# Gated attention and dropless experts on one core: two loads divided into column pieces

## The chip, the core and the metric

The kernel runs on one core of a Trainium2 chip. The core has a matrix engine, TensorE (PE), with a queue for weight loads (PEld); VectorE (DVE), ScalarE (ACT) and GpSimd (POOL); and SyncE (SP), which here does nothing but issue transfers. The engines run separate instruction queues in order and wait for each other through semaphores. The metric is the time of one execution on the device, in microseconds (us), and lower is better.

## What is computed

First a gated linear attention over a complex state, then a routed expert layer, top 1 of 8, all in float32:

```python
mag = np.sqrt(a_re * a_re + a_im * a_im)
scale = np.minimum(mag, 0.999) / (mag + 1e-06)
for t in range(S):                     # S = 768, B = 4, H = 8, D = 48
    new_re = ar * S_re - ai * S_im     # ar, ai: the scaled gates at t
    new_im = ar * S_im + ai * S_re
    S_re, S_im = new_re + k_t v_t^T, new_im
    y[:, :, t] = q_t S_re
x = y as (3072 tokens, 384)
logits = x @ w_gate                    # 8 experts
e = argmax(logits); g = softmax(logits)[e]
out = g * (relu(x @ w1[e]) @ w2[e])    # w1: 384 x 1024, w2: 1024 x 384
```

## The kernel before, in words

**Attention.** Time is cut into six stretches of 128 steps. Within a stretch the gates become cumulative decays and angles, and the recurrence becomes matrix products. Its stages are placed by hand-set priorities (the table WHEN), and a scheduler orders each engine's instructions from them. The fast path uses an approximation of the gates that holds only in a range: a_re above 0.61 and above |a_im|. So all gates are read a second time and tested.

**The range check** is `in_range(j)`, j = 0 to 5. A piece j is a tile of 128 rows by RW = 1536 columns of a_re and one of a_im (tile name `rc`; 768 KB each, 6 KB per row). Two reductions on DVE (line 926, output `junk`) read both tiles. The pool `rp` has two buffers of each tile, so piece j + 2 can be loaded only when both reductions of piece j are done. The results are used once, in `verdict()`, before the last expert. Piece j is called behind expert place j + 1 in the text, but the scheduler is free to put their transfers and reductions where it sees room. In the built program the first five rc transfers stand ahead of expert place 1's weights on SP's queue.

**Experts.** The eight experts are sorted by their number of tokens into "places" 0 to 7, with room for 448, 416, 416, 408, 400, 384, 376 and 360 tokens (CAPS). For each place:

- `load_w(i)` (lines 588 to 602) reads the expert's number and issues its weights on SP: `wa`, the first weights, 128 x 3 x 1024 elements, 1536 KB, and `wb`, the second, 1536 KB. For place 0 wa is one transfer over 128 rows. For places 1 to 7 it is four transfers of 32 rows each (384 KB, runs of 4 KB); the rows are permuted to suit a transpose of 32 x 32 blocks on DVE. wb has runs of 1.5 KB. There are two sets of buffers, even and odd places: wa of place i + 2 can go out when the first layer of place i is done, wb when its second layer is done. Place 1's weights wait until place 0's tokens have been turned ("rows first").
- `gather(i)` (line 616) collects the tokens' rows by indirect transfers that GpSimd issues (tile `xg`); `turn(i)` transposes them (on PE for place 0, line 646, on DVE for the others, line 636).
- `expert(i)` runs the first layer (matmuls into `hps`, eight h tiles of 128 columns of w1, 3 steps each, two matmul records per step), empties each PSUM tile with a ReLU, even h tiles on DVE (line 691), odd ones on ACT (line 689), in four PSUM buffers; then the second layer (matmuls into `yps`), the scaling by the gate on DVE (line 711), and `scatter`, an indirect write to the output by GpSimd (line 658).

Place 0 is in two parts: its first two token tiles run while attention ends; the rest, its tail of 192 columns, runs at about 298 us. Every transfer that SP issues carries one of eight semaphores in turn, and it is held until the transfer that used the same semaphore before it has landed. So at most eight are under way. If the range check fails or an expert has more tokens than its place holds, a general path runs; with these inputs it does not.

Of the kernel before, what the change touches and what calls it, by code (L numbers as in the profile page):

```python
# [17 lines left out]
SYNC = mybir.DependencyInfo(mybir.DependencyClass.Sync, mybir.DependencyReason.DATA)  # L18
# [6 lines left out]
T_MAX = 1.5  # L25
SQ = 1
Q4 = 32
CAPS = (448, 416, 416, 408, 400, 384, 376, 360)


# [8 lines left out]
def kernel(  # L39
# [12 lines left out]
    nc = tc.nc  # L52
# [4 lines left out]
    E, _, F = w1.shape  # L57
# [22 lines left out]
    def const(shape, name, dt=FP):  # L80
        return cp.tile(shape, dt, name=name)

    def iota(pattern, name, base=0, cm=0):
# [16 lines left out]
        out=last, in_=ones, pattern=[[0, P]], base=-(P - 1), channel_multiplier=1, compare_op=OP.is_ge, fill=0.0  # L100
# [26 lines left out]
    for a in range(4):  # L127
        nc.gpsimd.memset(quarter[a * Q4 : (a + 1) * Q4], float(a))

# [340 lines left out]
    caps = const([P, E], "caps")  # L470
    for i, c in enumerate(CAPS):
        nc.gpsimd.memset(caps[:, i : i + 1], float(c))
# [112 lines left out]
    def tiles(i):  # L585
        return -(-CAPS[i] // P)

    def load_w(i, after=None):
        o = own0 if i == 0 else owner[:, i : i + 1]
        ev = nc.sync.value_load(o[0:1, 0:1], min_val=0, max_val=E - 1)  # L590
        wa = EP[i % 2].tile([P, KD, F], FP, tag="wa", name="wa")
        parts = [(slice(0, P), w1[ds(ev, 1)].rearrange("o (k p) f -> p (o k) f", p=P))]
        if i >= SQ:
            w = w1[ds(ev, 1)].rearrange("o (a k j) f -> a j (o k) f", a=4, k=KD)
            parts = [(slice(a * Q4, (a + 1) * Q4), w[a]) for a in range(4)]
        for p, w in parts:
            ins = nc.sync.dma_start(out=wa[p], in_=w)
            if after is not None:
                tc.add_manual_dep(ins.ins, after.ins.name, SYNC, reason="rows first")
        wb = EP[i % 2].tile([P, KF, DM], FP, tag="wb", name="wb")  # L600
        nc.sync.dma_start(out=wb, in_=w2[ds(ev, 1)].rearrange("o (i p) d -> p (o i) d", p=P))
        T["w", i] = wa, wb

    def gather(i, t0, t1, rows=N):

        if t0 == 0:
            T["xg", i] = EP[i % 2].tile([P, CT * DM], FP, tag="xg", name="xg")
        c1 = min(CAPS[i], t1 * P)
        if i < SQ:
            view, w = xd[0:rows, :], DM  # L610
            parts = [(min(P, c1 - t * P), t, tok[:, i, t : t + 1]) for t in range(t0, t1)]
        else:
            view, w = xd.rearrange("n (a c) -> (n a) c", a=4), DM // 4
            parts = [(P, j, tok4[:, i, j // 4, j % 4 : j % 4 + 1]) for j in range(4 * t0, -(-c1 // Q4))]
        for m, (n, j, ap) in enumerate(parts):
# [12 lines left out]
    def turn(i, t0, t1, ps, end=None):  # L628

        xg = T["xg", i]  # L630
        if t0 == 0:
            T["xt", i] = EP[i % 2].tile([P, KD, CAPS[0]], FP, tag="xt", name="xt")
        c0, c1 = t0 * P, min(CAPS[i], t1 * P)
        if i >= SQ:
            j1 = -(-c1 // Q4)
            T["turned"] = nc.vector.transpose(
                out=T["xt", i][:, :, c0 : j1 * Q4].rearrange("p k (j s) -> p j k s", s=Q4),
                in_=xg[:, c0 // Q4 * (DM // 4) : j1 * (DM // 4)].rearrange("p (j k x) -> p j k x", x=Q4, k=KD),
            )
            behind(T["turned"], [T["held"]])  # L640
            return
        for d in range(KD):
            tp = ps.tile([P, 512], FP, tag="tp", name="tp")
            for t in range(t0, t1):
                n = min(P, CAPS[i] - t * P)
                ins = nc.tensor.transpose(
# [130 lines left out]
    for hp in range(HP):  # L777
        for i in range(2):
            nc.sync.dma_start(
                out=back[i * 64 : i * 64 + D, hp, DD:], in_=w_gate[hp * DD + i * D : hp * DD + (i + 1) * D, :]  # L780
# [84 lines left out]
    for g in range(NT):  # L865
        u, b = divmod(g, B)
        if b % HB == 0 and u + 1 < NU:
            put(g, load_qkv, u + 1, b // HB)
        if b in (1, 2) and u + 3 < NU:
            put(g, load_gates, u + 3, *HS[b - 1])  # L870
        if b == 0 and u in GROUPS:
            tc.cur_priority = 4000 + int((g + 1) * 200)
            T["second"] = route(*GROUPS[u])
        if u == NU - 1 and b == 0:
            gates_only.close()
            tc.cur_priority = 4000 + int((g + 1) * 200)
            T["second"] = route(NU - 2, NU - 1)
            put(g + 1, table, "natural_log_exp_and_others")
            put(g + 1, T["second"])
            put(g + 1, first_place)  # L880
            EP[0] = pool2("e0", 1, side="right", reuse_waits="tile")
            EP["y"] = pool2("y0", 2, side="right", reuse_waits="tile")
            put(g + 1, load_w, 0)
            put(g + 1, gather, 0, 0, EARLY, (NU - 1) * B * P)
        ahead(g)
        at(when("products"), products, g + 1) if g else None
        at(when("results0"), results, g, 0)
        at(when("results1"), results, g, 1)
        at(when("state"), state, g)
        at(when("evict"), evict, g)  # L890
        at(when("scores0"), scores, g + 1, 0)
        at(when("scores1"), scores, g + 1, 1)
        at(when("outer"), outer, g + 1)
        at(when("finish"), finish, g)
# [21 lines left out]
    RW = N * DM // P // NR_  # L916
    inr = const([P, 2 * NR_], "inr")

    def in_range(j):
        a = [rp.tile([P, RW], FP, tag=f"rc{i}", name=f"rc{i}") for i in range(2)]  # L920
        for t, src in zip(a, (a_re, a_im)):
            s = src.rearrange("b h t d -> (b h t d)").rearrange("(p f) -> p f", p=P)
            nc.sync.dma_start(out=t, in_=s[:, j * RW : (j + 1) * RW])
        junk = rp.tile([P, RW], FP, tag="junk", name="junk", bufs=1)
        for i, (op, sc) in enumerate(((OP.max, A_MIN), (OP.mult, -1.0))):
            stt(
                out=junk, in0=a[1], scalar=sc, in1=a[0], op0=op, op1=OP.is_lt,
                accum_out=inr[:, 2 * j + i : 2 * j + i + 1],
            )
# [19 lines left out]
    DRAINS = (3, 6)  # L949
    turn(0, EARLY, tiles(0), psG)  # L950
    load_w(1, T["turned"])
    for i in range(E):
        t0 = EARLY if i == 0 else 0
        if i == E - 1:
            verdict()
        if i + 1 < E:
            gather(i + 1, 0, tiles(i + 1))
        expert(i, t0, tiles(i), psH, psO, yp, (lambda: turn(i + 1, 0, tiles(i + 1), psG)) if i + 1 < E else None)
        if i in DRAINS:
            drain()  # L960
        if i + 2 < E:
            load_w(i + 2)
        if 1 <= i <= NR_:
            in_range(i - 1)
# [4 lines left out]
    with tc.If(nc.values_load(flag[0:1, 1:2], min_val=0, max_val=P * (NC + 1)) > 0):  # L969
# [16 lines left out]
        with tc.If(bad_gates > 0):  # L986
            with tc.tile_pool(name="fb", bufs=1) as fb:
# [8 lines left out]
                w = [fb.tile([P, TS, DG], FP, name=f"w{i}") for i in range(3)]  # L996
                yt = fb.tile([P, TS, D], FP, name="yt")
                yo = fb.tile([B * H, TS, D], FP, name="yo")
                with tc.For_i(0, S // TS, 1) as iv:
                    for i in range(4):  # L1000
                        sl = slice(i * B * H, (i + 1) * B * H)
                        for t, a in zip(src, (q, k, a_re, a_im)):
                            nc.sync.dma_start(
                                out=t[sl],
                                in_=a[:, :, ds(iv * TS, TS), i * DG : (i + 1) * DG].rearrange("b h t d -> (b h) t d"),
# [34 lines left out]
                    for b in range(B):  # L1040
                        nc.sync.dma_start(
                            out=xf[ds(iv * TS + b * S, TS), :].rearrange("t (h e) -> h t e", h=H),
                            in_=yo[b * H : (b + 1) * H],
# [134 lines left out]
        with tc.For_i(0, cnti, 1) as iv:  # L1178
            ev = nc.sync.value_load(gown[0:1, ds(iv, 1)], min_val=0, max_val=E - 1)
            wa = ro.tile([P, KD, F], FP, tag="wa", name="wa")  # L1180
# [8 lines left out]
                out=xg, out_offset=None, in_=xf[:, :], in_offset=bass.IndirectOffsetOnAxis(ap=ti, axis=0)  # L1189
# [13 lines left out]
            for f in range(KF):  # L1203
# [4 lines left out]
                out=out,  # L1208
                out_offset=bass.IndirectOffsetOnAxis(ap=ri, axis=0),
                in_=y,  # L1210
# [40 lines left out]
```

## Time and profile before

| | |
|---|---|
| runs | 563.99 us median of 3 (560.99 to 564.17) |
| the profiled execution | 561.03 us; its span 559.3 us |
| mean granted clock of TensorE | 0.991 |
| DMA, whole span | 73.49 MB in 167,735 packets, 131 GB/s |
| SP's queue of transfers | 162,792 packets, 63.12 MB, 52.4% of 16 engines' span |
| GpSimd's queue | 4,896 packets, 9.77 MB, 5.9% |
| wa: transfers | 28 of 384 KB and 1 of 1536 KB |
| rc: transfers | 12 of 768 KB |
| rc reductions on DVE | 12, median 1748 ns, from 292.3 to 443.2 us |

The span in forty slices of 14 us each; a digit is the busy share in tenths:

```profile
DVE  5378687788789888785565221251442412212210
ACT  6877988876588874553200010111101102000000
POOL 3000000000000000001058555707347064370101
PEclk9989989999999999999999999999999899999999
DMA  9977691938655826503468966753865444650001
```

Up to about 270 us it is attention, with all engines at work; then come the experts, where DVE and ACT are mostly idle and GpSimd gathers and scatters. The chain of work that ended last says the same by line: "PE yps L69 16.4%; PE hps L69 13.7%; issue 3.5%", of the part of it that can be followed back.

How to read it: an engine's busy share is an average over stages. PE's matmul ends are modelled, and a few records of evictions or matmuls may be missing. "remote" or "issue" as the releaser of a wait means that the profile shows nothing for it.

### The profile page before, as it was taken

Reading aid. Unit: us, or ns where it says so; the run is one execution under the profiler, and the core shown is the slowest. Engines: PE = TensorE matmul, PEld = TensorE weight load, DVE = VectorE, ACT = ScalarE, POOL = GpSimd, SP = SyncE. Lnnn points to the kernel's source line nnn. Section 1 sums busy time; section 2 is a strip of 40 time slices with the busy share of each in tenths; the row PEclk is TensorE's granted clock in tenths of the full one; section 3 lists DMA queues with packets and bytes.
Section 4 is the critical chain, followed back from the end, with each engine's and each line's share of the span. In section 5 each row is a group of like instructions: output and inputs, shape, how many; then the busy total and the mean of one; then the engine's idle time right before and its main releaser. Section 6 shows DMA issues by size and latency. Waiting matters only on the chain. (4 is left out here: it accounts for less than half of the span.)

```text
span 559.3 us, 8295 instructions
## 1 busy us (share of the span) xinstructions
PE 523.6 (94%) x3154; PEld 370.8 (66%) x3154; DVE 289.6 (52%) x585; ACT 214.3 (38%) x323; POOL 132.7 (24%) x161
## 2 busy tenths in 40 slices
PE   3889979999999999999998999899899899999996
PEld 3666858878888898888766555455454455555663
DVE  5378687788789888785565221251442412212210
ACT  6877988876588874553200010111101102000000
POOL 3000000000000000001058555707347064370101
PEclk9989989999999999999999999999999899999999
DMA  9977691938655826503468966753865444650001
GB/s 164 187 102 103 112 142 22 180 60 168 116 86 115 150 55 140 74 30 139 174 222 222 265 196 137 252 133 73 307 142 189 144 112 148 135 171 18 26 2 41
DMA packets 167735, 73.49 MB, mean 131 GB/s; under 512 B 149053, under 2 KB 160343, under 8 KB 167688
## 3 DMA queue, kind: packets, MB, share of 16 engines
q1 hardware_dynamic: 162792, 63.12, 52.4%
q0 software_dynamic: 4896, 9.77, 5.9%
q8 instruction: 27, 0.44, 0.3%
q14 instruction: 20, 0.16, 0.1%
HBM read 63.34 MB, written 9.73 MB: 131 GB/s over the span
## 5 line engine op out<-in xcount | busy, mean ns | idle before, releaser
L69 PE MATMUL hps<-xt,wa 128*128 128x416 f32 (+7 forms) x432 | 136.8, 472 | 8.8 <-issue 4.2
L69 PE MATMUL yps<-wb,ht 128*128 128x384 f32 (+6 forms) x464 | 134.1, 487 | 0.0
L69 PEld LDWEIGHTS hps<-xt,wa 128*128 128x128 f32 x432 | 79.9, 192 | 62.7 <-issue 32.0
L616 POOL DMA_INDIRECT xg<-xd,tok x92 | 94.8, 1030 | 88.5 <-PE tp L332 40.6
L69 PEld LDWEIGHTS yps<-wb,ht 128*128 128x128 f32 (+6 forms) x464 | 75.1, 175 | 55.8 <-issue 8.6
L689 ACT ACTIVATE ht<-hps 128x416 f32<-128x416 f32 (+7 forms) x36 | 16.7, 467 | 151.7 <-PE hps L69 103.9
L711 DVE TENSOR_SCALAR y<-yps,gate 128x384 f32<-128x384 f32 (+1 forms) x23 | 14.2, 618 | 93.2 <-PE yps L69 76.5
L658 POOL DMA_INDIRECT out_dram<-y,row x28 | 29.2, 1044 | 118.6 <-DVE y L711 100.9
L69 PE MATMUL at<-qt,kt 96*128 96x128 f32 x384 | 53.9, 280 | 0.7 <-DVE am L340 0.7
L691 DVE TENSOR_SCALAR ht<-hps 128x416 f32<-128x416 f32 (+7 forms) x36 | 18.8, 527 | 68.6 <-PE hps L69 41.8
L261 POOL DMA_DIRECT2D ai<-cd x4 | 3.4, 839 | 211.0 <-ACT R L175 100.6
L69 PEld LDWEIGHTS at<-qt,kt 96*128 96x128 f32 x384 | 47.7, 192 | 4.5 <-issue 1.1
L69 PE MATMUL yt<-am,v 128*48 128x128 f32 x384 | 42.7, 281 | 0.6 <-DVE am L340 0.6
L340 DVE TENSOR_TENSOR am<-at,tri 128x512 f32<-128x512 f32 x48 | 33.0, 688 | 18.6 <-PE at L69 18.5
L721 ACT COPY z<-yps 32x384 f32<-32x384 f32 (+3 forms) x13 | 6.1, 470 | 84.2 <-PE hps L69 58.0
L69 PE MATMUL yt<-qt,G 96*48 96x128 f32 x320 | 35.7, 274 | 0.0
L332 PE MATMUL tp<-ident,K 128*96 128x128 f32 x192 | 33.5, 284 | 1.3 <-DVE K L323 1.1
L69 PEld LDWEIGHTS dk<-v,K 128*96 128x96 f32 x320 | 32.9, 168 | 2.1 <-issue 1.0
L69 PE MATMUL dk<-v,K 128*96 128x48 f32 x320 | 33.5, 244 | 0.2 <-DVE G L371 0.2
L332 PE MATMUL tp<-ident,Q 128*96 128x128 f32 x192 | 33.4, 277 | 0.0
L334 ACT COPY kt<-tp 96x512 f32<-96x512 f32 x48 | 27.9, 581 | 11.0 <-PE tp L332 10.8
L334 ACT COPY qt<-tp 96x512 f32<-96x512 f32 x48 | 28.2, 587 | 4.2 <-PE tp L332 4.2
(170 smaller groups left out, 667.2 us busy)
## 6 DMA issues: line engine op xcount, KB each, us to landing
wb<-in_moe_w_dram SPq DMA_DIRECT2D x8, 1536.0 KB
wa<-in_moe_w_dram SPq DMA_DIRECT2D x28, 384.0 KB
q<-in_q_dram SPq DMA_DIRECT2D x12, 384.0 KB
k<-in_k_dram SPq DMA_DIRECT2D x12, 384.0 KB
v<-in_v_dram SPq DMA_DIRECT2D x12, 384.0 KB
xd<-x SPq DMA_DIRECT2D x24, 192.0 KB
rc<-in_a_re_dram SPq DMA_DIRECT2D x6, 768.0 KB
rc<-in_a_im_dram SPq DMA_DIRECT2D x6, 768.0 KB
```

The lines of the kernel that those rows point to most:

```text
L69: T["mm"] = nc.tensor.matmul(o, lhsT=lhsT, rhs=rhs, start=start, stop=stop, skip_group_check=True)
L261: nc.gpsimd.dma_start(out=T["ai", u][0:1, b0:b1].rearrange("p b h d -> p (b h d)"), in_=cd[1, u - 1 : u, b0 * DM : b1 * DM], accum_op=OP.add,)
L332: nc.tensor.transpose(out=tp[0:DD, j], in_=X[:, hg * 4 + j], identity=ident)
L334: nc.scalar.copy(out=t[0:DD], in_=tp[0:DD])
L340: tt(out=am, in0=at, in1=bc(tri, 1, 4), op=OP.mult)
L616: ins = nc.gpsimd.indirect_dma_start(out=T["xg", i][0:n, j * w : (j + 1) * w], out_offset=None, in_=view, in_offset=bass.IndirectOffsetOnA ...
L658: ins = nc.gpsimd.indirect_dma_start(out=out, out_offset=bass.IndirectOffsetOnAxis(ap=row[0:n, i, t : t + 1] if to is None else to[0:n], a ...
L689: nc.scalar.activation(out=ht[:, f, c0:c1], in_=ps, func=AF.Relu)
L691: T["held"] = ts(out=ht[:, f, c0:c1], in0=ps, scalar1=0.0, scalar2=None, op0=OP.max)
L711: ts(out=y[0:n], in0=ps[0:n], scalar1=g, scalar2=None, op0=OP.mult)
L721: nc.scalar.copy(out=z[j * w : j * w + n], in_=ps[j * w : j * w + n])
```

## The change

A constant CUT = 256 columns, 1 KB of float32, is introduced. Each wa transfer becomes four, one for each 256 of its 1024 columns; for places 1 to 7 the loop over column pieces is outside, the one over the four row groups inside, so all rows of the first 256 columns go before the next 256. Each rc transfer of 1536 columns becomes six. Every new wa transfer carries the same dependence on the turned rows, where there was one. The loads of wb, the buffers and all compute instructions are unchanged.

```diff
+CUT = 256
...
     def load_w(i, after=None):
...
-        for p, w in parts:
-            ins = nc.sync.dma_start(out=wa[p], in_=w)
-            if after is not None:
-                tc.add_manual_dep(ins.ins, after.ins.name, SYNC, reason="rows first")
+        for c in range(0, F, CUT):
+            for p, w in parts:
+                ins = nc.sync.dma_start(out=wa[p, :, c : c + CUT], in_=w[:, :, c : c + CUT])
+                if after is not None:
+                    tc.add_manual_dep(ins.ins, after.ins.name, SYNC, reason="rows first")
...
     def in_range(j):
...
-            nc.sync.dma_start(out=t, in_=s[:, j * RW : (j + 1) * RW])
+            for c in range(0, RW, CUT):
+                nc.sync.dma_start(out=t[:, c : c + CUT], in_=s[:, j * RW + c : j * RW + c + CUT])
```

The transfers per execution are then 116 for wa (98,304 bytes each for places 1 to 7, 384 KB for place 0) and 72 for rc (128 KB each).

## The prediction

> **What bounds the kernel now.** I read the busy shares first, then TensorE's (PE's) timeline from the first expert on, then SP's, because the edit lies in two loads that SP issues, and last the engines that empty PSUM. The page's first line names the bottleneck:
>
> ```profile
> PE 523.6 (94%) x3154; PEld 370.8 (66%) x3154; DVE 289.6 (52%) x585; ACT 214.3 (38%) x323; POOL 132.7 (24%) x161
> ```
>
> PE is busy 523.6 of 559.3 us, so a transfer counts only where PE waits for it, directly or through another engine. PE's timeline (start us, length us, engine, line, operation, tiles, shape, count; idle before it and what ended that):
>
> ```profile
> 290.66 0.27 PE L646 MATMUL tp<-ident,xg 128*128 128x128 f32 x1
> 291.72 0.74 PE L646 MATMUL tp<-ident,xg 64*128 64x64 f32 x3 [0.79 <-DMA xg<-xd,tok]
> 292.87 0.33 PE L646 MATMUL tp<-ident,xg 128*128 128x128 f32 x1 [0.41 <-issue]
> ...
> 316.81 17.03 PE L69 MATMUL hps<-xt,wa 128*128 128x416 f32 x48
> ```
> ```profile
> 422.70 10.34 PE L69 MATMUL hps<-xt,wa 128*128 128x400 f32 x30
> 435.35 8.01 PE L69 MATMUL hps<-xt,wa 128*128 128x400 f32 x18 [2.31 <-ACT ht L689]
> ...
> 460.18 9.95 PE L69 MATMUL hps<-xt,wa 128*128 128x384 f32 x30
> 471.48 6.07 PE L69 MATMUL hps<-xt,wa 128*128 128x384 f32 x18 [1.35 <-ACT ht L689]
> ...
> 492.87 15.32 PE L69 MATMUL hps<-xt,wa 128*128 128x376 f32 x48
> ```
>
> Place 1 (416 columns) runs its 48 first-layer matmuls without a gap in 17.03 us, place 6 (376) in 15.32. Place 4 (400) takes 20.65 us, 422.70 to 443.35 where the chain of waits starts its second layer; in proportion to place 1 it would be 16.4. So measured place 2 (350.68 to 369.91) loses 2.2 us, place 3 (386.75 to 405.87) 2.4, place 4 4.3, place 5 (460.18 to 477.55) 1.6: 10.5 us, the largest idle pool of the expert stages. None of it waits for weights. PSUM is emptied late:
>
> ```profile
> 434.79 0.90 ACT L689 ACTIVATE ht<-hps 128x400 f32<-128x400 f32 x2 [7.11 <-issue]
> ```
> ```profile
> 430.00:431.00 1.00, 1.00 (x5) 0.56 (x4) 0.93 (x3) 0.00 (x0) 0.69 (x2) 1.00 1.02 381
> ...
> 434.00:435.00 1.00, 0.00 (x0) 0.00 (x0) 0.18 (x1) 0.21 (x1) 0.00 (x0) 1.00 0.99 393
> ...
> 437.00:438.00 1.00, 1.00 (x2) 0.37 (x2) 0.19 (x1) 0.00 (x0) 0.00 (x0) 0.50 0.02 6
> ```
>
> ACT takes h tile 1 at 434.79, although six matmuls at 0.34 us each put its end near 426.8. In these rows (window; length; busy PE, weight load, DVE, ACT, POOL; granted clock; DMA share; GB/s) the DMA engines are full at 381 to 393 GB/s, PE stands still in 434 to 435, and afterwards its granted clock is 0.50. What is in flight is on SP's timeline:
>
> ```profile
> 283.89 0.45 SPq L923 DMA_DIRECT2D rc<-in_a_re_dram  x1
> 284.36 0.34 SPq L923 DMA_DIRECT2D rc<-in_a_im_dram  x1
> 284.76 0.42 SPq L923 DMA_DIRECT2D rc<-in_a_re_dram  x1
> ...
> 299.86 3.33 SPq L597 DMA_DIRECT2D wa<-in_moe_w_dram  x4
> ...
> 426.20 0.40 SPq L601 DMA_DIRECT2D wb<-in_moe_w_dram  x1
> 426.69 0.64 SPq L923 DMA_DIRECT2D rc<-in_a_re_dram  x1
> 427.38 0.43 SPq L923 DMA_DIRECT2D rc<-in_a_im_dram  x1
> 443.38 1.90 SPq L597 DMA_DIRECT2D wa<-in_moe_w_dram  x4
> ```
>
> Behind place 4's evictions lie wb (1536 KB) and a pair of gate pieces (768 KB each); behind place 5's only a wb. The evictions are late in both, longer where the gate pieces are.
>
> **The change part by part.** Bytes, buffers and arithmetic stay. *SP's instructions.* wa becomes 4 instead of 1 for place 0, and 16 instead of 4 for places 1 to 7: 87 more. The gate pieces become 72 instead of 12: 60 more. At 0.47 us apiece (1.90 / 4; the gate rows start 0.47 and 0.40 apart) that is 69 us more of SP, in an engine that mostly waits.
>
> *wa of places 1 to 7.* 16 x 0.47 = 7.5 us per load instead of 1.9. Here a rule speaks against the change. The row: four parts of 384 KB leave SP in 1.90 us, so several are under way at once. The Trainium skill, page "DMA: Bandwidth & Descriptors", section "Rules for kernel authors", says to use 1 MiB or more per DMA and that small ones pay mostly overhead; its fit in "Anatomy of one DMA" (taken on GpSimd's path) is 2.0 us plus bytes / 436e3. For a part of 98,304 bytes I estimate 2.23 us from it, 36 us for 16 in a row, the whole of a place (386.75 to 422.70): wa and wb would not fit, and the kernel would be slower by tens of us. But the program gives SP's transfers eight semaphores in turn and holds a transfer only until the eighth before it has landed: eight at a time make 36 / 8 = 4.5 us, below the 7.5 us of issue. I take the row. Slack covers 7.5 us everywhere: wa of place 3 starts at 333.87 and is needed at 386.75. The tightest is place 1: 299.86 + 7.5 + 2 = 309.4 against 316.81, and at the slow pace of its four parts (3.33 / 4 = 0.83) it ends at 315.2. wb of place 1 then leaves at 307.4 to 313.2 instead of 303.24; it is needed at 333.68. Cost 0.
>
> *Place 0.* Three more transfers put wb 1.2 us later, at 261.2; the x write behind it starts at 262.34 and the first use of wb is at 278.54. Cost 0.
>
> *Order.* In the built program the queues of PE, ACT and POOL keep their order. On SP the gate parts slide behind later loads: all but the first part of piece 2 still go behind place 3's load; piece 4's first buffer is free only when piece 2's reductions are done, and DVE now runs those behind place 3's transposition (near 409 instead of 369.75). SP stands there with wa of place 5 queued behind: 409.3 + 7 x 0.47 + 7.5 = 420, in place of 407.8; needed at 460.18, and wb of place 5 goes at 426.20 as before. Likewise wa of place 6 waits behind piece 5 for piece 3's reductions (near 446.8): 446.8 + 12 x 0.47 + 7.5 = 460, needed at 492.87, wb due at 462.33. Cost 0. On DVE the twelve reductions (1.75 us each) only change places; the pair between two evictions of place 5 is 3.5 us beside four PSUM buffers, so I cost it at 0; uncovered, 1 us.
>
> *PE's waits.* Each first layer now waits for its weights at four h tiles instead of one, on up to four or five semaphores. Nearest row: place 6 starts with a wait on four, and its 15.32 us against 17.03 x 376 / 416 = 15.4 show nothing. Value 0; upper bound, if each of some 24 new waits cost 0.1 us, 2.4.
>
> *The gather at 291.72.* The gate pieces 0 and 1 leave SP within 2 us (from 283.89) and fill the DMA engines while GpSimd's gather for place 0 is on its way; PE waits 0.79 us for it, and 0.41 behind it. In parts, SP releases 128 KB per 0.45 us, 291 GB/s, against the 381 to 393 that fill the engines, so the gather finds gaps. Between 0 and -1.2 us; I take -0.8. The part after: DVE's first reduction at 292.31 needs 12 parts: 283.89 + 12 x 0.45 + 2 = 291.3. Just in time.
>
> *Late evictions.* Gate parts beside place 4 shrink from two pieces to five parts (640 of 1536 KB; the rest waits for a buffer), beside place 3 from three pieces to two. Place 4 loses 2.7 us more than place 5, which has only wb: that is the most the gate pieces can be worth there. But wb, unchanged, is late-making alone. Bounds -4 and, if more transfers make it worse, +1.5; I take -1.0, nearer to place 5.
>
> Sum: -0.8 - 1.0 = -1.8 us. The profiled execution took 561.03 us (span 559.3), so it becomes 559.2. The median of the runs, 563.99, lies 2.96 above that execution; carried over, 562.2.
>
> **The rivals.** *Slower: SP's throttle starves the gate reduction.* The eight-in-flight rule bites if parts take more than about 0.6 us each. At the 0.83 seen for wa of place 1, the 24 parts from 283.89 end at 303.8 and land near 305.8. DVE's third reduction stands between the first two evictions of place 0's tail and would hold the queue from about 300 to 307.6; PE, with four PSUM buffers, stops near 305, and the fourth reduction (1.75 us) follows before the next eviction. Price 3 to 7 us, at 6 with the gather's gain lost: 570 in terms of the median. For it: the 3.33 us. Against it: 0.47 in every other row. It decides from 0.6 us per part.
>
> *Faster: the long runs are what makes PSUM late.* If 1 KB runs let GpSimd's gathers and the evictions through, places 2 to 4 fall to place 5's loss: 2.2 + 2.4 + 4.3 - 3 x 1.6 = 4.1, with 1.2 from the gather and 2.4 from place 0's tail, 298.49 to 308.83 (48 matmuls of 192 columns in 10.3 us, 7.9 in proportion to place 1): -7.7, 556.3. For it: place 4 against place 5. Against it: wb's rows of 1.5 KB are left as they are, and place 5 suffers without any changed transfer.
>
> *Nothing.* The edit is off PE's path altogether, and the losses are tied to what stays: 564.
>
> **How the numbers follow.** This kernel's runs spread from 560.99 to 564.17, so about 1% is what can be told from no change: below 558.4 faster, above 569.6 slower. The forecast and *nothing* together 0.55; the faster rival 0.20; slower 0.25, the throttle and unknown costs of 147 more transfers (PE's waits at their bound included). The range leaves out the tail of the faster rival beyond 555 and of the slower beyond 572; the likeliest case alone is 559 to 566.
>
> **What would show it.** Right: the 0.79 us behind the gather shrinks; gate parts start about 0.45 us apart; place 4's 20.65 us falls by one or two while place 5's 17.37 stays; no PE idle is ended by wa. Wrong: DVE idle ended by rc near 300 to 306, parts 0.8 us apart, or PE waiting on wa at place 1 (throttle); places 2 to 5 all near 16.5 us (faster rival); first layers of places 6 and 7 stretched (PE's waits).

## The result, and the profile after

The changed kernel took 579.38 us (median of 4 runs, 578.14 to 581.82) beside 563.89 us for the kernel before (4 runs, 560.99 to 564.17). It is slower by 15.5 us, outside the range of the prediction. The recorded ratio is 1.0389, 95% interval 1.0343 to 1.0435; this and all ratios below are taken from the record, which forms them from fast runs alone, and they need not equal the quotient of the medians beside them, which is 1.0275 here. So the slowdown is 2.7% by the medians and 3.9% by the recorded ratio. Later groups of runs, on four chips, give another result: there the same two kernels were within 0.6% of each other, four times out of four. The experiments are about what lies between the two.

The profiled execution of the changed kernel took 578.14 us (span 576.4), 17.1 us more than the one of before. First the page's busy line:

```profile
PE 529.9 (92%) x3154; PEld 374.4 (65%) x3154; DVE 289.3 (50%) x585; ACT 214.3 (37%) x323; POOL 132.7 (23%) x161
```

PE's share fell from 94% to 92% and its busy time rose by 6.3 us with the same 3154 instructions: it waits more, and part of the time it runs slower. The timeline of PE says where (start, length, line, operation, tiles, count; idle before it and what ended that):

```profile
291.01 0.94 PE L648 MATMUL tp<-ident,xg 128*128 128x128 f32 x4
299.65 0.47 PE L648 MATMUL tp<-ident,xg 128*128 128x128 f32 x1 [7.71 <-issue]
299.91 8.02 PE L70 MATMUL yps<-wb,ht 128*128 128x384 f32 x16
...
308.06 8.26 PE L70 MATMUL hps<-xt,wa 128*128 128x192 f32 x48
316.15 8.05 PE L70 MATMUL yps<-wb,ht 128*128 128x384 f32 x32
...
370.44 10.20 PE L70 MATMUL hps<-xt,wa 128*128 128x416 f32 x24 [3.55 <-issue]
...
483.72 10.93 PE L70 MATMUL hps<-xt,wa 128*128 128x384 f32 x24 [3.46 <-DVE ht L693]
```

The same places in the kernel before:

```profile
293.03 5.33 PE L69 MATMUL yps<-wb,ht 128*128 128x384 f32 x16
...
298.49 0.92 PE L69 MATMUL hps<-xt,wa 128*128 128x192 f32 x4
...
308.83 8.05 PE L69 MATMUL yps<-wb,ht 128*128 128x384 f32 x32
```

The first four transpositions no longer wait for the gather (before: 0.79 us). Then PE stands for 7.71 us, and the sixteen matmuls of the second layer take 8.02 us where they took 5.33. The tail of place 0 starts at 308.06 instead of 298.49. Of the 17.1 us, measured as differences of start times: 0.35 lies before 291, 9.2 between the transposition and the tail, the tail itself gives back 2.2 (8.09 us to its second layer instead of 10.34), place 1 adds 0.2, and the first layers of places 2 to 5 add 3.2, 0.8, 0.6 and 5.0. Places 6 and 7 take what they took.

What does PE wait for at 292? VectorE and ScalarE empty the transposition's PSUM tiles:

```profile
294.98 0.62 DVE L713 TENSOR_SCALAR y<-yps,gate 128x384 f32<-128x384 f32 x1 [8.15 <-remote]
297.13 0.36 DVE L655 COPY xt<-tp 128x192 f32<-128x192 f32 x1 [1.54 <-remote]
297.51 1.76 DVE L929 SCALAR_TENSOR_TENSOR junk<-rc,rc 128x1536 f32<-128x1536 f32 x1
```
```profile
299.27 0.32 ACT L655 COPY xt<-tp 128x192 f32<-128x192 f32 x1 [12.20 <-remote]
```

ACT idles for 12.20 us and copies at 299.27 a tile that PE had finished by 291.95. Nothing was ahead of it in its queue. VectorE too is idle when the tiles are ready. So neither engine is busy, nor is data missing; PE's signal that the matmuls are done arrives 4 to 7 us late. I call this a late signal. In the fourteen traces of groups C to F below, PE's semaphore (the counter by which it tells the other engines) moves 0.01 to 0.07 us after the matmul that it reports, every time; here it moves at 292.05, 293.52, 294.95, 297.11 and 299.25, for matmuls that were over by 291.95. The windows of the same stretch (busy PE, PEld, DVE, ACT, POOL; granted clock; DMA share; GB/s):

```profile
291.00:292.00 1.00, 0.94 (x5) 0.41 (x3) 0.00 (x0) 0.00 (x0) 0.77 (x1) 1.00 1.05 292
...
294.00:295.00 1.00, 0.00 (x0) 0.00 (x0) 0.02 (x1) 0.00 (x0) 0.84 (x1) 1.00 0.91 279
...
296.00:297.00 1.00, 0.00 (x0) 0.00 (x0) 0.00 (x0) 0.00 (x0) 0.69 (x2) 0.50 0.90 283
```

GpSimd issues gathers throughout (POOL 0.7 to 0.8 busy), SP's gate parts keep the DMA engines at 0.9 to 1.05, everything else stands. After three idle microseconds, at 295.1, PE's granted clock falls to 0.50 and stays there until 305.3. That covers 5.4 of the 8.02 us of the second layer; at half speed they cost 2.7 us, the whole difference to 5.33.

The same thing was in the trace of before, where the prediction read it as late emptying of PSUM: ACT's eviction at 434.79, 8 us behind its matmuls, and with it the pool of 10.5 us at places 2 to 5.

### The profile page after: what moved, and what is told of

It is laid out like the page before. It is cut to its first block, busy times and chain, and to the rows that moved or that the text cites. A ratio compares the mean times of both kernels' runs of the same rounds, so it can differ in the third digit from the quotient of the medians.

```text
span 576.4 us, 8677 instructions
## 1 busy us (share of the span) xinstructions
PE 529.9 (92%) x3154; PEld 374.4 (65%) x3154; DVE 289.3 (50%) x585; ACT 214.3 (37%) x323; POOL 132.7 (23%) x161
## 4 chain that ended last, share of the span: by engine, by line
PE 78%; DVE 5%; another core or an unknown queue 5%; issue 5%; DMA 4%; ACT 3%; POOLq 0%; SPq 0%; ACTq 0%; DVEq 0%
PE hps L70 22%; PE yps L70 20%; PE tp L333 7%; PE yt L70 7%; PE at L70 7%; PE dk L70 4%; PE cst L70 3%; PE xb L70 3%; PE csl L70 3%; PE warm L70 2%; DMA xd<-x 2%; DMA carry<-cd 1%; PE sp L70 1%; DMA out_dram<-y,row 1%
## 5 line engine op out<-in xcount | busy, mean ns | idle before, releaser
L70 PE MATMUL hps<-xt,wa 128*128 128x416 f32 (+7 forms) x432 | 140.5, 483 | 12.7 <-DVE ht L693 6.5
L70 PE MATMUL yps<-wb,ht 128*128 128x384 f32 (+6 forms) x464 | 136.8, 493 | 0.0
L70 PEld LDWEIGHTS hps<-xt,wa 128*128 128x128 f32 x432 | 82.2, 197 | 67.9 <-issue 36.5
L70 PEld LDWEIGHTS yps<-wb,ht 128*128 128x128 f32 (+6 forms) x464 | 76.5, 179 | 57.2 <-issue 11.0
```

The source lines that it names most:

```text
L70: T["mm"] = nc.tensor.matmul(o, lhsT=lhsT, rhs=rhs, start=start, stop=stop, skip_group_check=True)
```

## The experiments

Groups B to F ran on five different chips, each group on one, with its own runs of the kernel before; of A the chip is not known. Times are medians in us.

| group | kernel before | kernel | time | ratio (95% interval) |
|---|---|---|---|---|
| A, recorded | 563.89 | changed | 579.38 | 1.0389 (1.0343 to 1.0435) |
| B | 552.31 | wa_only | 562.78 | 1.012 (1.0029 to 1.0212) |
| | | rc_only | 559.82 | 1.0125 (1.0086 to 1.0163) |
| | | rc_runs | 553.50 | 1.0006 (0.997 to 1.0043) |
| | | hold | 556.00 | 1.0057 (1.0035 to 1.008) |
| C | 547.20 | changed (after_again) | 547.48 | 0.9995 (0.9971 to 1.002) |
| | | pause | 573.23 | 1.0455 (1.0405 to 1.0505) |
| | | pause2 | 563.46 | 1.0272 (1.0218 to 1.0325) |
| | | pause_cut | 547.83 | 1.0013 (0.9991 to 1.0035) |
| D | 547.46 | changed (after_third) | 547.48 | 1.0000 (0.9981 to 1.0019) |
| | | rc01_whole | 548.22 | 1.0021 (1.0 to 1.0041) |
| | | late_red | 546.88 | 1.0005 (0.9987 to 1.0024) |
| | | hold2 | 548.30 | 1.0022 (1.0005 to 1.0039) |
| E | 548.15 | changed (after_fourth) | 546.32 | 0.9945 (0.9915 to 0.9974) |
| | | late_red_b | 547.13 | 0.9978 (0.996 to 0.9996) |
| | | rc01_whole_b | 548.80 | 1.0005 (0.9979 to 1.003) |
| F | 547.79 | changed (after_fifth) | 547.38 | 0.9988 (0.9969 to 1.0006) |
| | | late_red_c | 547.93 | 0.9997 (0.9977 to 1.0018) |
| | | rc01_whole_c | 548.33 | 1.0002 (0.9975 to 1.0029) |

Late signals are in all six profiles of groups A and B and in none of the fourteen of C to F. The kernel before goes the same way: 563.9 and 552.3 us in A and B, 547.2 to 548.2 in the others. Against the first layers of after_again, where nothing is lost, places 2 to 5 of before lose 10.5 us in A and its tail of place 0 another 2.2 (10.34 against 8.09): 12.7 of the 16 us between A and the others. In rc_runs, whose places run as before's, B loses 5.1 at places 2 to 5 (the expectations below say 4.4, counted by proportion).

Two things about this split are open. The groups differ in more than the chip: A and B were run before 11:00 on one day, C to F after 11:30, so the hour fits as well as the chip. And the traces differ in more than PE's signals. Each gather or scatter that lands moves its semaphore sixteen times; of the 2000 such moves on GpSimd's transfers, the traces of C to F hold 1984 to 2000, those of A and B only 728 to 955. In the changed kernel's trace all semaphores together, those of SP's transfers included, have 46 records between 288 and 299.3, in bursts that begin mostly 0.7 us apart (292.03, 292.77, 293.49, 294.24, 294.93), and each of the five late signals lies in such a burst. after_again has 467 records in that stretch, no two more than 0.36 us apart. So it is not PE's signal alone that is held there. Whether semaphores were slow, or the recording of the trace itself had a part in it, the runs do not show; that engines stood still is seen without the semaphores, from the starts of their instructions.

### Group B: the parts of the change one by one

**wa_only**: only the first weights are cut. The edit is the first half of the change alone.

> Only the experts' first weights are cut; the gate pieces go in one transfer of 768 KB each, as before. Three theories share what is known: the changed kernel stands at 579.4 us against 563.9, and in its trace PE's second layer of place 0 begins 9.2 us later, because the evictions of the token transposition start late though PE's matmuls were long done; places 2 and 5 lose 3.2 and 5.0 us more in the same way, and place 0's tail gains 2.2. T1, the number of transfers that SP issues makes PE's signals late, whichever they are: no gate parts stand at 284 to 296, so the 9.2 us go, but the second layers of places 2 to 5 still lose about as in the changed kernel; 568 to 570. T2, short runs of 1 KB beside GpSimd's gathers make them late: wa's parts lie beside no gather for long, so near before, 562 to 566. T3, bulk over 128 rows in flight beside GpSimd's gathers, whatever its cut: SP's time before wb is what counts; near before, 561 to 567. Rival, the 87 more transfers of wa and PE's added waits cost by themselves: first layers of places 6 and 7 longer than 15.4 and 14.7 us, 570 or more.

Measured: 1.012, but with a wide interval (four runs, 556.20 to 568.76). Its profiled execution was the longest of the four, so no time is taken from it; but it does show where late signals are: at places 1 to 4, and none behind the transposition of place 0. The expectations were written on the baseline of 563.9; T1's 568 to 570 is a ratio of 1.007 to 1.011, T2's and T3's are 0.995 to 1.006, the rival's 1.011 and more. T1 and the rival fit, and the interval does not exclude the others. How much it loses at which place stays open.

**rc_only**: only the gate pieces are cut, the second half alone.

> Only the gate pieces are cut into six parts per tile; the first weights go as before. T1 (number of transfers) and T2 (1 KB runs): the 24 parts from 284 on stand beside place 0's gathers, so the second layer of place 0 begins near 300 instead of 292 and the kernel takes 573 to 582. T3 (any bulk over 128 rows beside gathers): the bulk is there in before too and did not delay these signals, so by T3 alone the cut does nothing, 562 to 566; if it is slow all the same, the theory needs the length of time that the bulk is in flight, which the parts stretch from 2 to 12 us of issue. Rival, SP's throttle (late data for DVE's reductions): slow too, but DVE's idle time between 292 and 306 is then ended by the rc transfers and not by PE.

Measured: 1.0125, 7.5 us; slower as T1 and T2 said, but by less than their 1.016 to 1.032. PE's timeline shows the stop of the changed kernel, at less than half its length:

```profile
293.40 0.93 PE L647 MATMUL tp<-ident,xg 128*128 128x128 f32 x4
297.65 0.48 PE L647 MATMUL tp<-ident,xg 128*128 128x128 f32 x1 [3.32 <-issue]
297.92 7.70 PE L70 MATMUL yps<-wb,ht 128*128 128x384 f32 x16
```

Idle for 3.32 us, then the second layer at the low clock: 7.70 instead of 5.33 us. Together 3.32 - 0.41 + 7.70 - 5.33 = 5.3 us, of the 7.5. The rival, late data for VectorE, is out: VectorE's wait in front of the copy was ended by PE, and its wait for gate data was 0.31 us.

**rc_runs**: one transfer for each gate tile, as before, but written into rows with gaps, so that every run is 1 KB. SP's order is before's.

```diff
-        a = [rp.tile([P, RW], FP, tag=f"rc{i}", name=f"rc{i}") for i in range(2)]
+        a = [rp.tile([P, RW // CUT, CUT + 16], FP, tag=f"rc{i}", name=f"rc{i}")[:, :, 0:CUT] for i in range(2)]
...
-            nc.sync.dma_start(out=t, in_=s[:, j * RW : (j + 1) * RW])
+            nc.sync.dma_start(out=t, in_=s[:, j * RW : (j + 1) * RW].rearrange("p (c f) -> p c f", f=CUT))
```

> The kernel before with each gate tile in one transfer, as before, but written into rows broken after every 1 KB (a gap of 64 bytes), so that a descriptor holds 1 KB as in the change while SP issues no transfer more. T2, short runs alone: the signals of PE at 291 to 300 are late as in the change, the second layer of place 0 begins 6 to 10 us later, 570 to 580. T1, number of transfers: as before, 561 to 566. T3: as before. This run tells the two halves of the cut apart.

Measured: 1.0006, as before. Its page counts 175,415 packets, 7,680 more than before (12 tiles of 128 rows, five more pieces each), so the runs were in fact short. PE's timeline:

```profile
291.65 0.73 PE L647 MATMUL tp<-ident,xg 64*128 64x64 f32 x3 [0.94 <-DMA xg<-xd,tok]
292.79 0.33 PE L647 MATMUL tp<-ident,xg 128*128 128x128 f32 x1 [0.41 <-issue]
292.96 5.33 PE L70 MATMUL yps<-wb,ht 128*128 128x384 f32 x16
```

No stop, no low clock, and the wait for the gather is there as in before. T2 is refuted for the gate pieces: what costs in rc_only is the division into transfers, or the times that it shifts, and not the length of the runs. The six traces of A and B agree on the place: behind the transposition PE stops in the two whose gate pieces are cut (changed, rc_only) and in none of the four where they are whole (before, wa_only, rc_runs, hold).

**hold**: nothing cut; wb of places 2 to 7 and all gate pieces wait on SP until a place's tokens have been transposed.

```diff
+            load_wb(i + 1, T["turned"])
...
+            tc.add_manual_dep(ins.ins, after.ins.name, SYNC, reason="gathers first")
```

> The kernel before (nothing cut) with the second weights of places 2 to 7 and the gate pieces held on SP until the tokens of the place have been gathered and transposed, so that no bulk over 128 rows is in flight while GpSimd gathers. T3: the late signals at places 2 to 5 are gone, each first layer takes its proportion of place 1 (16.4 us at place 4), up to 10 us less than before: 552 to 560. T1 and T2: the cause stays or was never there in before; 560 to 566. Rival: the held transfers come too late, PE waits on wb or wa at some place, 566 or more, and the wait is named by the trace.

Measured: 1.0057, slower. Half of T3 came true, and the other half refutes it:

```profile
297.10 0.92 PE L69 MATMUL hps<-xt,wa 128*128 128x192 f32 x4
300.07 3.52 PE L69 MATMUL hps<-xt,wa 128*128 128x192 f32 x20 [2.05 <-DVE xt L660]
307.80 5.85 PE L69 MATMUL hps<-xt,wa 128*128 128x192 f32 x24 [4.22 <-issue]
...
422.74 16.39 PE L69 MATMUL hps<-xt,wa 128*128 128x400 f32 x48
```

Place 4 takes 16.39 us, its proportion of place 1, and places 2, 3 and 5 lose nothing either. But the tail of place 0, 48 matmuls, lasts from 297.10 to 313.65. The cause is late signals again, and SP's timeline and a window of the same kernel show that they need neither a cut nor a bulk transfer:

```profile
272.47 0.32 SPq L389 DMA_DIRECT2D xd<-x  x1
300.04 4.50 SPq L597 DMA_DIRECT2D wa<-in_moe_w_dram  x4
```
```profile
298.00:299.00 1.00, 0.02 (x1) 0.00 (x0) 0.06 (x1) 0.00 (x0) 0.85 (x1) 1.00 0.21 49
```

From 272.8 to 300.04 SP issues nothing. PE's second layer ended at 296.97, and VectorE takes its tile at 298.94. DMA carries 49 GB/s there, the gathers alone. The tile of the transposition ended at 297.17 and is taken at 299.65. So neither SP's transfers (T1) nor bulk in flight (T3) is needed for late signals; the second stop, 4.22 us before 307.80, has four parts of wa beside it, so that they may lengthen it is not excluded. What the late signals read here have in common is that GpSimd is gathering or scattering, or has stopped within the last 3 us.

### Group C: is it the unbroken run of gathers?

A new theory, T4, rested on before's trace: at places 2 to 5 the first late signal comes about 11 us into a run of 14 to 16 indirect transfers (gathers, with scatters between them) 1.3 us apart, and the last ones arrive together about 2 us after the run. The pause kernels break these runs.

```diff
+            if i >= 1 and m and m % 4 == 0:
+                tc.add_manual_dep(ins.ins, last.ins.name, SYNC, reason="pause")
+            last = ins
```

In pause2 the first line reads `if i >= 2 and m and m % 2 == 0`; pause_cut is the changed kernel with the lines of pause.

> The changed kernel once more, so that it stands beside the other runs on one chip: the kernel before took 552.3 us in the runs of wa_only, rc_only, rc_runs and hold, 563.9 in the first ones. If the loss is the same thing everywhere, the ratio to before is again near 1.039, or near the sum of the halves, 1.012 + 1.0125, which is 1.025. PE's second layer of place 0 begins 6 us or more later than in before.

> The kernel before, with nothing cut, where from place 1 on every fourth of GpSimd's gathers waits until the one before it has landed. New theory T4: PE's signals are late when GpSimd has issued gathers without a gap for some 9 us or more (in the trace of before the first late signal stands about 11 us into each run of 14 to 16 gathers, with no bulk in flight; they come all together about 2 us after its last gather), whatever SP does meanwhile. By T4 a gap after four gathers keeps the signals in time: places 2 to 5 lose under 2 us together instead of about 4.4 (measured in rc_runs, whose places run as before's), 1 to 4 us faster than before. T1, number of SP's transfers, and T3, bulk in flight: no change, within 1 us. Rival: the gathers end too late for the transposition of the next place, slower, and PE's idle time stands in front of a first layer.

> As pause, but every second gather waits, from place 2 on; place 1's gathers run as in before. T4: the signals at places 2 to 5 are as good as never late, 2 to 5 us faster than before, and place 0's tail is as in before. If every fourth is not enough of a gap and every second is, the gap's length is what counts. T1, T3: no change. Rival: gathers too late, slower.

> The changed kernel (all cut) with the pause after every fourth gather from place 1 on. T4: the stop of PE behind the token transposition of place 0 shrinks, since place 1's gathers no longer run without a gap from 283 to 300; the second layer of place 0 begins under 3 us later than in before, places 2 to 5 lose less than 3 us together, and the kernel stands within 1% of before. T1 (24 transfers from SP are what delays PE's signals): the 6 to 9 us at 291 to 300 stay, and the kernel as slow as the changed one.

Measured: the surprise is after_again, 0.9995. Its PE timeline is what the prediction hoped for, and more:

```profile
289.19 0.94 PE L648 MATMUL tp<-ident,xg 128*128 128x128 f32 x4
290.53 0.33 PE L648 MATMUL tp<-ident,xg 128*128 128x128 f32 x1 [0.41 <-ACT xt L655]
290.70 5.33 PE L70 MATMUL yps<-wb,ht 128*128 128x384 f32 x16
...
296.16 8.26 PE L70 MATMUL hps<-xt,wa 128*128 128x192 f32 x48
...
346.10 17.03 PE L70 MATMUL hps<-xt,wa 128*128 128x416 f32 x48
...
413.51 16.39 PE L70 MATMUL hps<-xt,wa 128*128 128x400 f32 x48
...
446.72 15.75 PE L70 MATMUL hps<-xt,wa 128*128 128x384 f32 x48
```

The same instructions, the same indirect transfers in runs of 15 to 17, the same parts on SP, and every first layer runs without a gap. No late signal, hence nothing for T4 to gain: an unbroken run of gathers is not enough to make signals late. Whether pauses would help where signals are late stays untested. Here they gain nothing: pause and pause2 are slower, pause_cut is as fast as before. In pause the gathers come too late for the transposition, as its rival said; first PE's, then POOL's row:

```profile
320.17 19.77 PE L69 MATMUL hps<-xt,wa 128*128 128x416 f32 x48 [6.76 <-DVE xt L640]
```
```profile
366.37 0.99 POOL L617 DMA_INDIRECT xg<-xd,tok  x1 [5.97 <-DMA xg<-xd,tok]
```

A gather issued at 359.35 behind wb and two gate pieces (SP at 356.93 to 358.43, 3 MB) had landed only at 366.37, 7 us later. In pause_cut, where wb alone stood there, the corresponding wait was 2.65 us, and that kernel lost nothing (1.0013).

### Groups D to F: does the cost go with the late signals?

T5: by itself the cut costs nothing; what it costs is the late signals, on chips that have them. Three more groups, on three more chips, looked for one that has them, to tell there which part matters. In rc01_whole the gate pieces 0 and 1 stay in one transfer each and all else is cut. In late_red nothing is cut, but the reductions of these pieces stand behind place 0's tail. hold2 is hold without holding these pieces.

The core of the three edits, in this order:

```diff
+            cut = RW if j < 2 else CUT
+            for c in range(0, RW, cut):
```
```diff
+            if j < 2:
+                behind(ins, [T["held", 0]])
```
```diff
-            tc.add_manual_dep(ins.ins, after.ins.name, SYNC, reason="gathers first")
+            if j >= 2:
+                tc.add_manual_dep(ins.ins, after.ins.name, SYNC, reason="gathers first")
```

> The changed kernel a third time. Its ratio to before was 1.0389 in the first runs and 0.9995 in those of after_again, where the trace shows no late signal of PE at all, in before's long runs of gathers neither. New theory T5: by itself the cut costs nothing (0 to 0.3%), and what it costs is the late signals, which are there on some chips and not on others. Then the time of before tells which it is: near 547 for before, no late signal and a ratio of 0.997 to 1.003; at 552 and above for before, late signals, and a ratio of 1.015 to 1.045. If the ratio does not go with the time of before, T5 is wrong.

> The changed kernel with the first two pairs of gate pieces in one transfer each, as in before; the other gate pieces and the first weights stay cut. Where before is at 552 or above: by T1 (number of parts on SP) and by T5 alike the stop at 291 to 300 goes, so 6 to 9 us less than the changed kernel; what it still loses at places 2 to 5, 3 to 8 us, is wa's and the later pieces'. Where before is near 547: the same as before, within 1.5 us.

> The kernel before, nothing cut; only VectorE's four reductions of the gate pieces 0 and 1 stand behind the last eviction of place 0's tail, so that from 285 to 306 nothing of them runs beside GpSimd's gathers (in before two stand near 292 to 296, two at 299 to 303, and gathers beside them take 1.5 to 2.2 us instead of 1.0). T5 with T4: where before is at 552 or above, the signals at 297 to 308 come late as they do in hold, where too no reduction ran and SP had issued nothing for 15 us; the tail of place 0 takes over 12 us instead of 8 to 10. T1: the tail only gains, 0 to 2 us faster, for its evictions no longer stand behind reductions. Where before is near 547: T1's answer, 0 to 2 us faster.

> As hold, but gate pieces 0 and 1 are not held, so their loads and reductions stand beside place 0 as in before; wb of places 2 to 7 and pieces 2 to 5 wait for the transposition. In hold places 2 to 5 lost nothing (16.39 us for place 4), but the tail of place 0 lost 6 us. Where before is at 552 or above: both gains together, 3 to 8 us faster than before. Where before is near 547: nothing to gain, within 1.5 us; if it is slower there, the held transfers cost by themselves.

> The changed kernel beside the kernel before once more, to find out what goes with the ratio. T5: where before takes 545 to 548, no late signal of PE and a ratio of 0.997 to 1.003; where before takes over 551, late signals, 6 us or more lost between 291 and 300, and a ratio of 1.015 to 1.045.

> Nothing cut, the four reductions of pieces 0 and 1 behind place 0's tail. On a chip where before has late signals (over 551 us): by T4 they become later at 297 to 308, for nothing slows GpSimd's gathers there, and the kernel is 2 to 8 us slower than before; by T1 (SP's number of transfers is what makes them late) it is as fast as before or up to 2 us faster. On a chip without late signals: as before, within 1.5 us, as in late_red.

> The changed kernel with gate pieces 0 and 1 whole. On a chip with late signals: the stop of PE behind the token transposition (9.2 us in the first runs) is gone and the ratio to before 1.00 to 1.02; if the stop is there all the same, it was not the 24 parts. On a chip without late signals: 0.998 to 1.004, as in rc01_whole.

> The changed kernel beside before again, on whatever chip it falls. T5: before at 545 to 548 and a ratio of 0.993 to 1.003 without late signals, or before over 551 with them and a ratio of 1.015 to 1.045.

> Nothing cut, four reductions behind place 0's tail. With late signals on the chip: T4 says late at 297 to 308, 2 to 8 us slower than before; T1 says 0 to 2 us faster. Without them: within 1.5 us of before.

> All cut but gate pieces 0 and 1. With late signals on the chip: no stop of PE between 291 and 300 and a ratio of 1.00 to 1.02 if the 24 parts make the stop; the stop is there otherwise. Without them: 0.998 to 1.004.

Measured: the kernel before took 547.5, 548.2 and 547.8 us, no profile has a late signal, and the changed kernel stands at 1.0000, 0.9945 and 0.9988. T5's 0.997 to 1.003 for such chips held in D and F; in E the change is a little faster than that. The other kernels keep to what was expected for such chips, within 1.5 us of before. late_red, which has all transfers of before, shows that without any cut nothing is lost at places 2 to 5 there either (of the kernel before itself only A has a trace):

```profile
291.50 0.27 PE L646 MATMUL tp<-ident,xg 128*128 128x128 f32 x1
292.40 0.73 PE L646 MATMUL tp<-ident,xg 64*128 64x64 f32 x3 [0.63 <-DMA xg<-xd,tok]
...
416.52 16.39 PE L69 MATMUL hps<-xt,wa 128*128 128x400 f32 x48
```

The wait for the gather, 0.63 us, is there where gate pieces 0 and 1 are whole (0.62 to 0.69 in the three rc01_whole kernels) and gone in all four profiles of the changed kernel in C to F. That is one of the two gains of the prediction, at nearly its size; in the whole time of the kernel it cannot be told from noise.

None of the three chips has late signals, so the other half of the question was not answered: on a chip that has them, rc01_whole and late_red would say whether the 24 parts of pieces 0 and 1 make the loss of 9.2 us, or the shift of VectorE's reductions, beside which GpSimd's gathers take 1.5 to 2.4 us instead of 1.0. A third candidate is the number of semaphore moves: sixteen for each landed transfer make 752 for SP's transfers behind 283 us before the cut and 3056 after it (47 and 191 transfers), beside 1904 for GpSimd's. It fits a stop that comes with more transfers, and hold, where the gathers alone go with late signals; no run tests it. And no version beat both kernels: hold2 stands at 1.0022, and the gain of hold at places 2 to 5 exists only where signals are late.

## Why the prediction was wrong, by its steps

**Late evictions, taken as -1.0 with bounds of -4 and +1.5: this step failed.** In the recorded runs the loss from late signals, low clock included, grew by 9.2 us behind the transposition of place 0, where the prediction had put nothing, and by 3.2 + 0.8 + 0.6 + 5.0 = 9.6 us at places 2 to 5. The prediction saw the loss (10.5 us at places 2 to 5, ACT at 434.79), called it late emptying of PSUM, and put it down to transfers in flight, because place 4 with gate pieces lost more than place 5 without. It then let the price scale with the bytes of gate pieces. Its own rows spoke against that: place 3 had three pieces in flight and lost 2.4 us, place 4 two and lost 4.3. hold shows late signals at 49 GB/s with SP silent for 27 us, and rc_runs none behind the transposition, at 314 GB/s in 1 KB runs, so bytes are not what they follow. And it treated the 10.5 us as the kernel's own. In groups C to F they are zero, with the same instructions: they belonged to the conditions of the recorded runs. What makes the signals late, and why the cut makes them later, stays open. An effect of unknown cause that already costs 10 us cannot be given an upper bound of 1.5, and it is not bound to the places where it was last seen.

**The gather at 291.72, taken as -0.8: right, and overrun in the recorded runs.** The wait of 0.79 us is gone in all five profiles of the changed kernel, and rc01_whole shows that it is the cut of pieces 0 and 1 that takes it away. That the gather finds gaps between the parts is not shown: in 291 to 292 us the DMA engines are at a share of 1.05, at 292 GB/s where the prediction worked out 291. Behind the four transpositions stood the stop of 7.71 us, where the prediction had only 0.41.

**The rival with the right place and the wrong cause.** The slower rival put 6 us at 300 to 306, through SP's throttle and starved reductions. Its test was named: parts 0.8 us apart, VectorE's idle time ended by rc. Neither happened. SP took 0.45 to 0.56 us for a part:

```profile
284.25 2.71 SPq L926 DMA_DIRECT2D rc<-in_a_re_dram  x6
287.07 3.33 SPq L926 DMA_DIRECT2D rc<-in_a_im_dram  x6
```

and the reduction at 297.51 started without a wait, behind a copy that PE's late signal had held up. In after_again, without late signals, the first reduction starts at 291.44 after 1.17 us of waiting for its data; the prediction said 291.3, just in time. The sign came out as this rival said, for a reason that stood on the list only as "unknown costs of 147 more transfers".

**SP's instructions, order, PE's added waits, all taken as 0: right.** Sixteen parts of wa take 8.0 to 9.1 us at places 3 to 7 in after_again, against 7.5 worked out; PE's matmuls wait for neither wa nor wb, in the recorded profile or in after_again, but for one wait of 0.2 us there. First layers of places 6 and 7 take 15.32 and 14.77 us in the traces of before, the changed kernel and after_again, so the added waits are free. The weighing of the rule from the Trainium skill (page "DMA: Bandwidth & Descriptors", section "Rules for kernel authors": 1 MiB or more per transfer, and mostly overhead under 64 KB, which these parts of 96 and 128 KB are above) against the row of 0.47 us came out for the row: in C to F 147 more transfers show no cost.

**The sum.** -1.8 us was 0.3% of the kernel. On the four chips without late signals the changed kernel measures -0.3, 0.0, -3.0 and -0.7 us against before by the recorded ratios (C to F: ratio less 1, times the time of before), and +0.3, 0.0, -1.8 and -0.4 by the medians. Three of the four intervals include no change at all. So "within 1%" holds there and the small gain is not shown; of its two terms only the gather's was there to be had, and a value near -1.8 in E is luck. In the recorded runs it missed by 17 us (579.4 against 562.2).

## What to carry to other kernels

When an eviction starts microseconds after its matmuls ended, its engine was idle and its data was there, read the signal as late, and count that time as unexplained: price it from zero to several times its size, and do not let it follow the bytes in flight. Before a change is costed against such a pool, look whether the pool is there in runs on other chips and at other times; here it was 10.5 us in the recorded runs, 5.1 in group B and nothing on four chips. And a change that measures 3 to 4% slower in one group and equal in four has been shown to be slower only under the condition of the first: say what is known of it.

## What the runs showed of the hardware

- PE's semaphore moved up to 8 us after its matmuls ended, during or shortly after runs of gathers, in two groups of six; in the other four it followed within 0.07 us. Ends of matmuls are modelled, but starts are not: in before the last matmuls of four h tiles start 2.0 us apart, and the tiles are signalled at 434.72, 434.79, 434.87 and 434.94; in hold those of three tiles, 0.97 us apart, at 308.14, 308.22 and 308.30. So the work was done and the signal was held. Where PE waited for another engine there, it went on at once: at 299.65 after ScalarE's copy that ended at 299.59, in hold at 307.80 after VectorE's eviction that ended at 307.75. Why, and what frees the signals, is open.
- In these two groups the traces hold 728 to 955 of 2000 semaphore moves of GpSimd's transfers, against 1984 to 2000 in the others.
- Standing still was paid twice: in the changed kernel PE's granted clock fell to 0.50 3.1 us after the last matmul, and sixteen matmuls took 8.02 us (7.70 in rc_only) instead of 5.33.
- A gather behind 3 MB of whole transfers took 7 us to land (pause), where the quickest took 2.4 in the same trace.
